# Attention scores in column halves, gate logits in column quarters, and a different schedule of bulk transfers, in a fused attention and mixture-of-experts kernel

## The chip, the cores and the metric

The kernel runs on one core of one Trainium2 chip. The metric is the device time of one execution in microseconds (us). A core has five engines that run side by side: TensorE (PE, matrix products; its weight loads are counted apart as PEld), VectorE (DVE), ScalarE (ACT), GpSimd (POOL) and SyncE (SP, which issues transfers and does no arithmetic). Sixteen DMA engines move data between the large memory and the on-chip memory. TensorE takes two instructions for every product, a weight load (LDWEIGHTS) of the stationary operand and a MATMUL that streams the moving operand past it. A product of 32-bit numbers takes two such pairs, which can be seen from the counts: 256 score products are 512 MATMUL and 512 LDWEIGHTS records in the profile.

## The reference, cut to what matters

```python
# attention: 4 batches, 8 heads, 768 positions, 64 numbers per head, 8 memory slots
for c in range(24):                       # chunks of 32 queries
    keys = mem_k ++ k[32c-16 : 32c+40]    # clipped to the sequence
    a = softmax(q[32c : 32c+32] @ keys.T / 8)
    x[chunk] = a @ (mem_v ++ v[32c-16 : 32c+40])
# experts: x is (3072, 512); 8 experts, 512 -> 1024 -> 512
logits = x @ w_gate
expert = argmax(logits); gate = softmax(logits)[expert]
for e in range(8):
    tok = tokens of expert e; if more than 80, keep the 80 with the largest gate
    out[tok] = gate[tok] * (relu(x[tok] @ w1[e]) @ w2[e])     # all other rows are zero
```

At most 640 of the 3072 output rows are not zero, so the kernel first writes zeros to all rows and later overwrites the chosen ones.

## The kernel before, in words

**Attention.** The work is 32 units. A unit is one pair of heads and one half (384 queries) of the sequence of one batch. Four units make a round: 384 tokens with all 512 numbers. One pass of the loop at line 852 computes, in this order on TensorE: the scores of the *next* unit (`scores`, line 773), a transposition of a key or query pair that is needed later (`turn_k`, `turn_q`), one step of the ranking of an earlier round (`later`), the transposition of the last unit's result (`turn_x`), and the products with the values (`values`, line 351, in 32-column pieces). The scores of a unit are two mask products (line 779) and 4 groups x 2 heads of products with 64 rows, 128 columns of weights and 96 moving columns (line 786). ScalarE takes their exponential (line 794).

**Ranking.** After every fourth unit, `Ranks.steps` gives a list of 11 small steps that are spread over the next passes. The first ones are the gate: `weigh` (line 387, four products that give partial logits per 128 numbers, then a copy by ScalarE, line 417), `logits` (line 422, three products that add up the partial logits), `gates`. For the last round `early` (line 810) computes the logits straight from the transposed results as they appear.

**Experts.** `run_experts` (line 997) gathers the 80 rows of each expert by an indirect transfer that POOL issues (line 1008), transposes them, and does `up` (line 1043) and `down` (line 1057) for each expert: 64 float products each, in 64-column halves of the weights, then scales and scatters the result (`store`, line 1111).

**Transfers.** SP issues nearly all transfers, in program order. In each pass it issues the loads of keys, queries and values (values six passes ahead), every fourth pass a store of a round's results, and then two *pieces* of bulk data of 256 KB: weights (`slow`) or zeros (`nothing`). Weights of an expert's layer are 8 pieces. Nine layer buffers exist; the layers 0, 1, 3, 4 and 2 (the last into the room that keys and queries used) are loaded in the loop, 40 pieces, and all 24 pieces of zeros too. Bulk starts at pass 4. After the loop `paced` issues the other layers; at most six pieces are in flight, so each piece waits for the sixth before it. `in_order` pins the order of every engine to the order of the program.

## Time and profile before

| | |
|---|---|
| three timed runs | 250.19, 251.43, 253.89 us (median 251.43) |
| profiled execution | 248.27 us, of which the span from first to last instruction is 246.5 us |
| attention (to the last transposition of a result) | ends at 138.4 us of the span |
| ranking of the last round, first expert's input | 138.4 to 150.9 us |
| experts | 150.9 to 246.5 us; last product at 240 us |
| bulk weights after the loop | 88 pieces of 256 KB, issued from 138.1 to 218.8 us |

The page gives busy time, shares and counts of each engine; the groups of instructions give for each line the count, the summed busy time and the mean of one in ns, and what the engine waited for just before. A wait on "issue" is a wait for which the profile shows no semaphore. The timeline gives start and duration in us. In a window's line stand the width, then for each engine the busy time and in brackets the number of instructions, the TensorE clock (1.00 is full), the share of the DMA engines and the rate in GB/s. Queue 8 ("instruction") carries the instructions themselves, in transfers of 16,384 bytes each.

### The profile page before, as it was taken

The numbers are of one execution on the slowest core, as the hardware profiler recorded it, in microseconds if no ns is written. First come the engines' busy times: TensorE is split into PE (matmuls) and PEld (weight loads), VectorE is DVE, ScalarE is ACT, GpSimd is POOL, SyncE is SP. The second block draws the span as 40 slices with busy tenths as digits, with TensorE's granted clock in tenths as the row PEclk, the third lists the DMA queues.
The fourth block names the chain that finished last, engine by engine and source line by source line (L and its number), as shares of the span: only waits on it lengthen the run. The fifth ranks groups of instructions, "written<-read, shape, count | busy, mean of one in ns | idle before, by whom it ended". The sixth has DMA issues, their size and how long they took to land. (4 is left out here: it accounts for less than half of the span.)

```text
span 246.5 us, 11417 instructions
## 1 busy us (share of the span) xinstructions
PE 228.3 (93%) x4976; PEld 200.6 (81%) x4976; DVE 105.5 (43%) x288; ACT 81.8 (33%) x198; POOL 80.5 (33%) x182
## 2 busy tenths in 40 slices
PE   5979999999999999999899999969799997999980
PEld 3857889798888788888778889959799996999970
DVE  3333447758579477585555862000112111110240
ACT  2245555665555573665545301100000101010000
POOL 2454947537275182450412147300101010110111
PEclk9999999999999999999999889989999999999996
DMA  6999999999999999999999899999999998890101
GB/s 205 284 283 298 279 296 325 340 370 321 341 364 330 376 331 334 370 278 329 302 305 372 264 363 307 295 333 298 311 335 313 358 288 284 277 332 28 32 29 37
DMA packets 69879, 70.97 MB, mean 288 GB/s; under 512 B 38204, under 2 KB 46396, under 8 KB 69820
## 3 DMA queue, kind: packets, MB, share of 16 engines
q1 hardware_dynamic: 67836, 67.17, 87.4%
q0 software_dynamic: 1024, 2.62, 3.5%
q8 instruction: 41, 0.67, 1.2%
q10 hardware_dynamic: 960, 0.36, 0.6%
q14 instruction: 18, 0.15, 0.2%
HBM read 56.24 MB, written 13.89 MB: 285 GB/s over the span
## 5 line engine op out<-in xcount | busy, mean ns | idle before, releaser
L794 ACT ACTIVATE P<-sp 128x384 f32<-128x384 f32 x64 | 27.9, 488 | 29.6 <-PE sp L786 29.6
L1043 PE MATMUL hp<-xn,w 128*64 128x80 f32 x896 | 33.7, 233 | 3.0 <-issue 3.0
L1043 PEld LDWEIGHTS hp<-xn,w 128*64 128x64 f32 x896 | 32.1, 137 | 3.9 <-issue 3.4
L786 PEld LDWEIGHTS sp<-qT,kT 64*128 64x128 f32 x512 | 33.2, 189 | 1.5 <-issue 0.9
L786 PE MATMUL sp<-qT,kT 64*128 64x96 f32 x512 | 33.5, 269 | 0.9 <-ACT qT L316 0.4
L1057 PE MATMUL yt<-hT,w 128*64 128x80 f32 x896 | 34.2, 239 | 0.0
L1057 PEld LDWEIGHTS yt<-hT,w 128*64 128x64 f32 x896 | 33.0, 142 | 1.2 <-issue 1.1
L1047 ACT ACTIVATE hT<-hp 128x320 f32<-128x320 f32 x16 | 7.0, 437 | 70.7 <-PE hp L1043 70.7
L1111 POOL DMA_INDIRECT out_dram<-y,idx_s x7 | 6.4, 917 | 73.0 <-DVE y L1110 73.0
L357 PE MATMUL o<-vw,P 128*32 128x65 f32 x1536 | 28.9, 222 | 0.7 <-issue 0.7
L357 PEld LDWEIGHTS o<-vw,P 128*32 128x32 f32 x1536 | 23.5, 109 | 6.3 <-issue 5.4
L346 DVE COPY kT<-pt 128x480 f32<-128x480 f32 x32 | 19.9, 666 | 16.3 <-PE pt L343 8.2
L268 POOL COPY vw<-mv 8x512 f32<-8x512 f32 x32 | 22.4, 703 | 8.7 <-DMA vw<-in_v_dram 8.7
L1022 DVE COPY xn<-xp 128x320 f32<-128x320 f32 x7 | 3.4, 491 | 39.4 <-PE xp L1020 39.4
L366 DVE TENSOR_TENSOR xr<-o,over_s 128x384 f32<-128x384 f32 x32 | 17.8, 558 | 1.1
L316 ACT COPY qT<-pt 128x384 f32<-128x384 f32 x31 | 16.0, 582 | 4.8 <-PE pt L315 4.8
L377 ACT COPY xT<-xt 128x384 f32<-128x384 f32 x32 | 15.7, 489 | 4.7 <-PE xt L375 4.7
L330 POOL COPY kh<-ld 128x768 f32<-128x768 f32 x15 | 12.3, 822 | 13.7 <-PE more L549 8.3
L375 PE MATMUL xt<-ident,xr 128*128 128x128 f32 x96 | 16.5, 281 | 0.0
L315 PE MATMUL pt<-ident,qh 128*128 128x128 f32 x96 | 15.0, 291 | 1.2 <-DVE kT L346 1.2
L1063 DVE COPY ys<-yt 128x320 f32<-128x320 f32 x7 | 3.4, 492 | 28.7 <-PE yt L1057 28.7
L531 DVE SCALAR_TENSOR_TENSOR less<-gbs,gw,behind 128x384 bf16<-128x384 f32 x21 | 15.0, 745 | 0.0
(162 smaller groups left out, 305.2 us busy)
## 6 DMA issues: line engine op xcount, KB each, us to landing
w<-in_moe_w_dram SPq DMA_DIRECT2D x120, 256.0 KB, 5.2
vw<-in_v_dram SPq DMA_DIRECT2D x60, 128.0 KB, 5.3
ld<-in_k_dram SPq DMA_DIRECT2D x16, 384.0 KB, 5.6
ld<-in_q_dram SPq DMA_DIRECT2D x16, 384.0 KB, 6.4
xd<-xr SPq DMA_DIRECT2D x8, 768.0 KB, 5.8
out_dram<-zero SPq DMA_DIRECT2D x24, 256.0 KB, 4.9
ld<-in_moe_w_dram SPq DMA_DIRECT2D x8, 256.0 KB, 6.0
vw<-in_v_dram SPq DMA_DIRECT2D x4, 96.0 KB, 5.6
```

The lines of the kernel that those rows point to most:

```text
L268: nc.gpsimd.tensor_copy(self.vw[n, f][:MS, :, :, :D], self.mv[b][:, h : h + 2].unsqueeze(2).to_broadcast([MS, 2, NG, D]),)
L315: nc.tensor.transpose(pt[:, t, :], qh[:, t0 + t].rearrange("p e d -> p (e d)"), ident)
L316: out[t0 // 3](qT.rearrange("p (x t) -> p x t", t=T0)[:, :, t0 : t0 + 3], pt.rearrange("p t x -> p x t"))
L346: nc.vector.tensor_copy(win[:, :, :, u0 : u0 + 3], _ap(pt, 0, [pt.ap[0], [JG, G], [1, (WK - MS) // T0], [step, 3]]),)
L357: nc.tensor.matmul(out[32 * i : 32 * i + 32, e, t, :], lhsT=P[e][:, g, CHUNK * c : CHUNK * c + CHUNK], rhs=self.vw[n, f][:, e, g, :], star ...
L366: nc.vector.tensor_tensor(out=xr[:, :, 128 * c : 128 * c + 128].rearrange("p t (e d) -> p e t d", e=2), in0=o[:, :, :, :D], in1=over_s[:, ...
L375: nc.tensor.transpose(xt[:, 128 * t : 128 * t + 128], xr[:, t, 128 * c : 128 * c + 128], ident)
L377: nc.scalar.copy(xT, xt[:, :HT])
L786: nc.tensor.matmul(sp[e][:, g], lhsT=at.kT[n][r, NG * f + g, :], rhs=at.qT[n][r, HT * f + GQ * g : HT * f + GQ * g + GQ], start=False, sto ...
L794: nc.scalar.activation(P[i][e], sp[e], Act.Exp, scale=scale)
L1043: nc.tensor.matmul(hp[j : j + 64, f, :], lhsT=w1[:, c, f1 : f1 + 64], rhs=xns[e][:, c, :], start=c == 0, stop=c == DK - 1,)
L1057: nc.tensor.matmul(yt[j : j + 64, d, :], lhsT=w2[:, f, d * 128 + j : d * 128 + j + 64], rhs=hTs[e][:, f, :], start=f == 0, stop=f == FK - 1,)
```

## The change

1. `scores`: each score product and each mask product is cut into two products with 64 columns of weights each, so that four products (two heads by two column halves) stand side by side.
2. `logits` takes the place of `weigh` and the old `logits`: for each of 3 token groups and 4 parts of the 512 numbers, four products with 32 columns of weights (transposed results) and 8 moving columns (`w_gate`), added up in PSUM. The copy by ScalarE, the tile `lus` and the constant `sel4` go. `gates` becomes a step of its own. `early` is cut into 32-column products in the same way.
3. Pieces have a size now. A layer's `w1` is 4 pieces of 512 KB (4 KB to a partition), `w2` 8 of 256 KB, and the zeros 12 of 512 KB (4 KB to a partition). `paced` counts sizes and keeps at most six units of 256 KB in flight, as before.
4. The bulk in the loop starts at pass 1, with two units a pass; one of six pieces is zeros. Six of the twelve pieces of zeros are left for after the loop, where they are issued ahead of the weights.
5. The lines that queue layer 2 at pass 26 stand twice, so its 2 MB are loaded twice into the same room.
6. Of the gathers, those of experts 1 to 3 are issued at the start of the experts, the others one by one after each `down`.

```diff
+    def paced(piece):
+        size, dma = piece
         dma()
-        pieces.append(list(nc.cur_bb.bb.instructions)[-1])
-        if len(pieces) > 6:
-            tc.add_manual_dep(pieces[-1], pieces.popleft().name, follow, reason="pieces")
+        ins = list(nc.cur_bb.bb.instructions)[-1]
+        last = None
+        while sum(n for n, _ in pieces) + size > 6:
+            last = pieces.popleft()[1]
+        if last is not None:
+            tc.add_manual_dep(ins, last.name, follow, reason="pieces")
+        pieces.append((size, ins))
...
-                lambda c=c, f=f: nc.sync.dma_start(
-                    t[:, c, f : f + 512], src[i // 2, c * 128 : c * 128 + 128, f : f + 512]
-                )
+                (FK // nch, lambda c=c: nc.sync.dma_start(
+                    t[:, c, :], src[i // 2, c * 128 : c * 128 + 128, :]
+                ))
                 for c in range(nch)
-                for f in range(0, DK * F // nch, 512)
...
-        def weigh(self, xTs, lu):
-            gate_parts(xTs, lu)
-            nc.scalar.copy(self.lus, lu[:, :HT])
-
-        def logits(self):
-            lp = self.ps("lp")
+        def logits(self, xTs, lp):
             for t in range(NT):
-                nc.tensor.matmul(
-                    lp[:, E * t : E * t + E], lhsT=self.lus[:, 128 * t : 128 * t + 128], rhs=sel4,
-                    start=True, stop=True,
-                )
+                for c in range(HP):
+                    for j in range(0, 128, 32):
+                        nc.tensor.matmul(
+                            lp[j : j + 32, E * t : E * t + E], lhsT=xTs[c][:, 128 * t + j : 128 * t + j + 32],
+                            rhs=wgc[:, c, :], start=c == 0, stop=c == HP - 1,
+                        )
             self.largest(lp)
...
-            for e in range(2):
-                r = slice(64 * e, 64 * e + 64)
+            quarters = [(e, slice(64 * e, 64 * e + 64), slice(h, h + 64)) for e in range(2) for h in (0, 64)]
+            for e, r, h in quarters:
                 nc.tensor.matmul(
-                    sp[e].rearrange("p g q -> p (g q)"), lhsT=mkey[r, f, :], rhs=mqry[r, f, :],
+                    sp[e][h].rearrange("p g q -> p (g q)"), lhsT=mkey[r, f, h], rhs=mqry[r, f, :],
                     start=True, stop=False,
                 )
             for g in range(NG):
-                for e in range(2):
-                    r = slice(64 * e, 64 * e + 64)
+                for e, r, h in quarters:
                     nc.tensor.matmul(
-                        sp[e][:, g], lhsT=at.kT[n][r, NG * f + g, :],
+                        sp[e][h, g], lhsT=at.kT[n][r, NG * f + g, h],
                         rhs=at.qT[n][r, HT * f + GQ * g : HT * f + GQ * g + GQ], start=False,
                         stop=g == NG - 1,
                     )
...
             if i == NU - 6:
                 slow += W.load(WR0)
-            for _ in range(2 if i >= 4 else 0):
-                bulk = slow if slow and (i >= NU - 6 or i % 4 < 3) else nothing
-                if bulk:
-                    bulk.popleft()()
-            for _ in range(2 if i >= 20 and i % 2 == 0 else 0):
-                if nothing:
-                    nothing.popleft()()
+            if i == NU - 6:
+                slow += W.load(WR0)
+            if i >= 1:
+                due += 2.0
+            while due > 0 and (slow or len(nothing) > 6):
+                turn = slow if slow and (moved % 6 < 5 or len(nothing) <= 6) else nothing
+                size, dma = turn.popleft()
+                dma()
+                due -= size
+                moved += 1
...
-        for e in range(1, E):
+        for e in range(1, 4):
             gather(e)
...
             down(e)
+            gather(e + 4)
```

More of the change, by code (lines that the diff above doesn't have):

```diff
@@ L115 @@
     tok = masks[:, 2 * WK + 2 * HT :].rearrange("p (i m) -> p i m", i=2)
-    wgc = const.tile([128, HP, 32], F32, name="wgc")
-    sel4 = const.tile([128, E], F32, name="sel4")
+    wgc = const.tile([128, HP, E], F32, name="wgc")
     identb = const.tile([128, 128], BF16, name="identb")
@@ L131 @@
     over_s = const.tile([128, NU, 2, NT], F32, name="over_s")
-    zero = const.tile([128, DM], F32, name="zero")
+    zero = const.tile([128, 2 * DM], F32, name="zero")
     xg0 = const.tile([cap, DM], F32, name="xg0")
@@ L160 @@
     pieces = deque()
-    def paced(dma):
+    def paced(piece):
+        size, dma = piece
         dma()
-        pieces.append(list(nc.cur_bb.bb.instructions)[-1])
-        if len(pieces) > 6:
-            tc.add_manual_dep(pieces[-1], pieces.popleft().name, follow, reason="pieces")
+        ins = list(nc.cur_bb.bb.instructions)[-1]
[5 more added lines that the diff above has]
+        pieces.append((size, ins))
     class Weights:
@@ L184, in load @@
             return [
-                lambda c=c, f=f: nc.sync.dma_start(
-                    t[:, c, f : f + 512], src[i // 2, c * 128 : c * 128 + 128, f : f + 512]
-                )
+                (FK // nch, lambda c=c: nc.sync.dma_start(
+                    t[:, c, :], src[i // 2, c * 128 : c * 128 + 128, :]
+                ))
                 for c in range(nch)
-                for f in range(0, DK * F // nch, 512)
             ]
     def zeros():
-        zrows = 128
+        zrows = 256
         return [
-            lambda i=i: nc.sync.dma_start(
-                out[i * zrows : (i + 1) * zrows, :].rearrange("(p r) d -> p r d", p=128),
-                zero.unsqueeze(1),
-            )
+            (2, lambda i=i: nc.sync.dma_start(
+                out[i * zrows : (i + 1) * zrows, :].rearrange("(p r) d -> p (r d)", p=128), zero
+            ))
             for i in range(N // zrows)
@@ L381, in store @@
             nc.sync.dma_start(xd[r * HT : r * HT + HT, :].rearrange("(t p) d -> p t d", p=128), xr)
-    def gate_parts(xTs, lu):
-        for c in range(HP):
-            nc.tensor.matmul(
-                lu[32 * c : 32 * c + 32, :HT], lhsT=wgc[:, c, :], rhs=xTs[c], start=True, stop=True
-            )
     full = [128, NT, E]
@@ L399, in __init__ @@
             tiles = dict(
-                lus=([128, HT], F32), lmax=([128, NT], F32), lg=(full, F32), first=(full, F32),
+                lmax=([128, NT], F32), lg=(full, F32), first=(full, F32),
                 best=([128, NT], F32), el=(full, F32), oh=([128, NT, 4, E], BF16), gw=([128, NT], F32),
@@ L413, in ps @@
             return self.ps_t.tile([128, 512 if kind == F32 else 1024], kind, name=name, tag="t")
-        def weigh(self, xTs, lu):
-            gate_parts(xTs, lu)
-            nc.scalar.copy(self.lus, lu[:, :HT])
-        def logits(self):
-            lp = self.ps("lp")
-            for t in range(NT):
-                nc.tensor.matmul(
-                    lp[:, E * t : E * t + E], lhsT=self.lus[:, 128 * t : 128 * t + 128], rhs=sel4,
-                    start=True, stop=True,
-                )
+        def logits(self, xTs, lp):
+            for t in range(NT):
+                for c in range(HP):
[4 more added lines that the diff above has]
+                        )
             self.largest(lp)
@@ L608, in turn_table, with steps @@
             nc.scalar.copy(self.tabT, tp[: 3 * E, :cap])
-        def steps(self, r, xTs, lu):
+        def steps(self, r, xTs, lp):
             def fifth():
@@ L628, in steps @@
             return [
-                lambda: self.weigh(xTs, lu), lambda: (self.logits(), self.gates()), lambda: None,
+                lambda: self.logits(xTs, lp), self.gates, lambda: None,
                 lambda: (self.spread(), self.parts(r)), fifth, sixth, seventh,
@@ L730 @@
         make_identity(nc, ident)
-        nc.gpsimd.memset(wgc, 0.0)
-        nc.scalar.dma_start(wgc[:, :, :E], moe_w_gate.rearrange("(c p) e -> p c e", p=128))
+        nc.scalar.dma_start(wgc, moe_w_gate.rearrange("(c p) e -> p c e", p=128))
         def for_gates():
@@ L738, in for_gates @@
             by_q = ident.rearrange("p (q r e) -> p r e q", q=4, e=E)[:, 0]
-            nc.vector.tensor_reduce(sel4, by_q, axis=AX, op=Alu.add)
             with nc.allow_low_precision("ones and zeros"):
@@ L770 @@
         units = [(HP * b + c, f) for b in range(B) for f in range(2) for c in range(HP)]
-        P, o, xr, xTs, lus = {}, {}, {}, {}, {}
+        P, o, xr, xTs = {}, {}, {}, {}
         def scores(i):
@@ L809, in early @@
                 for t in range(NT):
-                    nc.tensor.matmul(
-                        lp[:, E * t : E * t + E], lhsT=xTs[HP * (NR - 1) + c][:, 128 * t : 128 * t + 128],
-                        rhs=wgc[:, c, :E], start=False, stop=c == HP - 1 and t == NT - 1,
-                    )
+                    for j in range(0, 128, 32):
+                        nc.tensor.matmul(
+                            lp[j : j + 32, E * t : E * t + E],
+                            lhsT=xTs[HP * (NR - 1) + c][:, 128 * t + j : 128 * t + j + 32], rhs=wgc[:, c, :],
+                            start=False, stop=c == HP - 1 and t == NT - 1,
+                        )
         turns = {0: [("k", 2), ("q", 2)], 1: [("k", 3), ("q", 3)]}
@@ L820 @@
             turns[i + 1] = turns.get(i + 1, []) + [("q", n)]
-        later, done = deque(), deque()
+        later, due, moved = deque(), 0.0, 0
         ranks = Ranks(gt, ps_x)
@@ L873 @@
             if i and i % HP == 0:
-                lus[r] = ps_x.tile([128, 512], F32, name="lu", tag="t")
-                steps = ranks.steps(r - 1, [xTs[i - HP + c] for c in range(HP)], lus[r])
+                lr = ps_x.tile([128, 512], F32, name="lr", tag="t")
+                steps = ranks.steps(r - 1, [xTs[i - HP + c] for c in range(HP)], lr)
                 later = deque(
@@ L908 @@
         assert not slow
-        for dma in nothing:
-            paced(dma)
+        for piece in nothing:
+            paced(piece)
         r = NR - 1
@@ L1160 @@
             at.turn_mem(ps_t.tile([128, 512], F32, name="pm2", tag="t"))
-            for dma in zeros():
+            for _, dma in zeros():
                 dma()
@@ L1210 @@
                     at.store(r, xr)
-                    steps = ranks.steps(r, xTs, ps_l.tile([128, 512], F32, name="lu2", tag="l"))
+                    steps = ranks.steps(r, xTs, ps_l.tile([128, 512], F32, name="lr2", tag="l"))
                     for step in steps[: None if r < NR - 1 else 4]:
@@ L1228 @@
             for i in range(2):
-                for dma in W2.load(i):
+                for _, dma in W2.load(i):
                     dma()
```

## The prediction

> **What bounds the kernel now.** I read the page first (engines, queues, groups), then the timeline of TensorE pass by pass, then windows for the data rate, and last the waits and what came just before each idle stretch of TensorE.

> ```profile
> PE 228.3 (93%) x4976; PEld 200.6 (81%) x4976; DVE 105.5 (43%) x288; ACT 81.8 (33%) x198; POOL 80.5 (33%) x182
> q8 instruction: 41, 0.67, 1.2%
> L786 PEld LDWEIGHTS sp<-qT,kT 64*128 64x128 f32 x512 | 33.2, 189 | 1.5 <-issue 0.9
> L786 PE MATMUL sp<-qT,kT 64*128 64x96 f32 x512 | 33.5, 269 | 0.9 <-ACT qT L316 0.4
> ```

> TensorE is the bound: the next engine is busy half as long. For the scores the weight loads (33.2 us) take as long as the products. In the timeline one pass reads:

> ```profile
> 112.94 0.34 PE L779 MATMUL sp<-masks 64*128 64x384 bf16 x2
> 113.11 1.03 PE L786 MATMUL sp<-qT,kT 64*128 64x96 f32 x16
> 114.07 0.88 PE L315 MATMUL pt<-ident,qh 128*128 128x128 f32 x6
> ...
> 116.01 0.89 PE L357 MATMUL o<-vw,P 128*32 128x65 f32 x48
> ```

> There is no gap: passes follow each other with TensorE full. The few gaps are of one kind, and they matter here:

> ```profile
> 122.82 0.65 PE L357 MATMUL o<-vw,P 128*32 128x65 f32 x30 [0.73 <-issue]
> 162.84 0.35 PE L1043 MATMUL hp<-xn,ld 128*64 128x80 f32 x2 [2.28 <-issue]
> 175.33 0.49 PE L1043 MATMUL hp<-xn,w 128*64 128x80 f32 x7 [1.28 <-issue]
> 206.59 1.47 PE L1043 MATMUL hp<-xn,w 128*64 128x80 f32 x36 [1.74 <-issue]
> ```

> They fall in the middle of a group, and no semaphore is behind them. Counting TensorE's instructions in the trace (loads, products, semaphore instructions, some 10,060), the four gaps stand before numbers 4801, 6337, 6849 and 8385, all 193 above a multiple of 256. Queue 8 has 41 transfers of 16,384 bytes, one for each 256. So **TensorE runs out of instructions**. The trace's records of queue 8 give three times for each block: from its first instruction to the start of the transfer that brings the next block, 2.35 us on average over the 21 blocks of the attention (2.45 in the experts); the transfer, 1.09 us; and, at the four gaps, from its end to the next instruction, 1.46, 1.55, 1.24 and 1.37 us (1.4). A block thus can't be passed in less than about 2.35 + 1.09 + 1.4 = 4.84 us while data traffic is heavy. The work in a block is now 5.77 us in the attention (21 blocks from 18.7 to 139.8 us), so the refill hides; in the experts it is 4.4 to 5 us, and it hides only sometimes.

> ```profile
> 80.00:100.00 20.00, 19.76 (x389) 16.40 (x381) 12.26 (x34) 11.03 (x28) 7.87 (x17) 1.00 1.11 346
> 220.00:230.00 10.00, 10.00 (x280) 9.72 (x277) 1.24 (x2) 0.87 (x2) 1.22 (x2) 1.00 0.21 69
> ```

> The first row (last numbers: DMA share 1.11, 346 GB/s) is heavy traffic. In the second the refill starts 0.0 to 0.8 us after its block begins, not 2.4: the wait is for the data transfers.

> [...] here the six loads of line 422 (0.19 us each, 0.76 us for the six) follow each other at 113 ns. [...] 128 products with 64-column weights in 4.65 us, 36 ns apart.

> **The change part by part**, against the profiled execution (248.3 us; its span is 246.5; the median of the runs is 3.1 us above it, so I add the differences to 251.4).

> *Scores in halves.* Now 16 products of a unit start in (1.03 - 0.19) / 15 = 56 ns steps, the pace of the loads with two row halves in parallel. After, 32 with 96 columns: 36 ns x 96 / 80 = 43 ns for two column halves, 22 ns with both row halves, 0.70 us in place of 0.90. Gain 0.2 us x 32 = 6.4 us (from 0, if the tiles don't load in parallel, to 9). The mask products stay at 0.17 us.

> *Logits in quarters.* Now 0.79 us (line 387 to what follows) plus 0.67 us (line 422) a round. After, 96 products at the 14 ns of line 357's 32-column ones: 1.35 us. At the densest stretch of 256 instructions in the trace, 14.6 ns each, its 192 instructions take 2.8 us. So -0.1 to +1.3 us a round; I take 0. `early`: three parts, 3.06 us, become 1.4: gain 1.5 us, 0.4 of it in the ranking of the last round. ScalarE's copy (0.48 us x 7) lies beside TensorE: 0.

> *Instructions.* Each float product is four, each mask product two. Scores: +8 x 4 + 2 x 2 = 36 a unit, 1152. Logits: 48 products for 7, +164 a round, 1148. `early`: +144. Sum 2444, **9.5 blocks more**, nearly all in the attention: 30.5 blocks where there were 21. Their work is 121.1 - 1 (its gap) - 6.4 - 1.5 = 112 us, 3.7 us a block, which is below the refill. What a block takes is then the larger of the two. As a test, drawing measured refills against the measured work of each block gives 122.0 us for the attention before (121.1 measured) and 65.1 for 12 blocks of experts (65.7 measured). For after it gives 148 us with the refills as they are. But a slower attention moves its data at a lower rate, and the refill shortens: in the first four blocks, near 299 GB/s, it is 2.0 + 1.14 + 1.4 = 4.54 us. At 4.6 us a block 30.5 blocks are 140.3 us: **+19 us** (bounds: -8 if the refill hides, +27 with no relief).

> *Bulk in the loop.* 40 pieces of weights and 24 of zeros become 48 units (8 of them layer 2's second load) and 12: 60 for 64. A pass moves 384 KB of keys or queries, 256 of values, 512 of bulk and 192 of stores, 1.376 MB. In 3.9 us that is 353 GB/s; at 4.4 us 313. So data don't bind if the refill does. SP's second load of layer 2 must wait for the first (landing takes about 6 us); behind it in SP's queue stand only two stores. Bulk in passes 1 to 3 puts 1.5 MB (4 us of traffic) ahead of keys and values, where POOL already waited 3.7 us for keys at 23.7 us: 0 to 2, I take +0.5.

> *Zeros behind.* 88 pieces at 0.916 us each now; layer 14 has landed by 138.1 + 80 x 0.916 + 5.2 = 216.6 us and is needed at 223.5. Twelve units ahead cost 11 us: 4 us late, unless larger packets lift 286 GB/s to the attention's 345 (then on time). I take +2 (0 to +5). They land long before the first scatter (177.8 us).

> *Gathers.* 957 ns of POOL each; the later ones stand behind a scatter that waits for VectorE. Expert 5's is free after the scatter at 178 us and is read at 208: 0.

> Sum: +19 + 0.5 + 2 - 0.5 (`early` in the last ranking, rounded up) = +21; 251.4 + 21 = **272 us**.

> **Rivals.** (a) *Refill as now hidden*, PE bound: if refills came as promptly as at 220 us (0.8 + 1 + 1.4 = 3.2 us, below 3.7), the gain of 6.4 + 1.5 stays and zeros cost 2: 245.5. For it: before, 20 of 21 attention blocks hid theirs. Against: the 4.84 us. It decides below 3.7 us a block. Chance 0.12. (b) *Data rate takes the gain*: a pass of 3.6 us needs 382 GB/s, and 340 was the mean from 40 to 120 us; then attention stays near its length, 248 to 254. Needs short refills too: 0.13. (c) *Late weights*, larger packets slowing the paced stream, refills half hidden: +5 to +9, 256 to 260. 0.12. (d) Forecast, 0.63: 260 to 286; its top has refills without relief, with TensorE's clock halved after long gaps (after the 2.28 us gap line 1057 took 6.29 us, not 4.65). That the loads don't split [...] would show in the counts; it only removes the gain.

> **Numbers.** Two per cent, about what a measurement of this kernel tells from no change, is 246.4 to 256.5 us. Faster: (a) for the most part, 0.11. Same: (b) and a rest, 0.13. Slower: 0.76. Range 248 to 286, which leaves out (a) and the far top; the likeliest alone 260 to 286.

> **What would show it.** Right: about 50 transfers on queue 8; gaps "issue" in most blocks of the attention, some 0.5 to 1.5 us each; score groups of 0.75 to 0.9 us; the last transposition of a result near 158 us; attention's rate near 310 GB/s. Wrong: no such gaps although the counts rose, then (a) or (b), told apart by waits of POOL or TensorE for keys and values; or a wait for weights at line 1043 late in the experts, then (c).

## The result, and the profile after

The changed kernel takes 291.27 us (median; 289.52 to 293.43) against 250.81 (249.89 to 253.89) for the one before on the same chip: a ratio of 1.161, with a 95% interval of 1.150 to 1.171. The forecast was 272 us, 248 to 286. The direction was right, the size was not. Executions of one kernel differ by up to some 5%, part of them being slower at a lower clock (before, in the set of a_merge: 244.29 us at a mean clock of 0.989, 255.59 at 0.950); ratios with an interval, here and below, compare the faster ones. The profiled execution took 289.52 us (span 287.6, mean TensorE clock 0.921 where it had been 0.978). All stages below are in us of the span.

| stage | before | after | difference |
|---|---|---|---|
| attention, to the end of the last transposition of a result | 138.4 | 171.7 | +33.3 |
| ranking of the last round, to the first expert's first product | 12.5 | 13.6 | +1.1 |
| experts, to the last product | 89.1 | 94.8 | +5.7 |
| last scatter and end | 6.5 | 7.5 | +1.0 |

The page of the changed kernel first: engines, the TensorE clock in 40 slices of 7.2 us, the instruction queue.

```profile
PE 234.3 (81%) x6198; PEld 205.1 (71%) x6198; DVE 104.5 (36%) x287; ACT 79.1 (27%) x191; POOL 79.3 (28%) x181
PEclk9999879999959999779789689999999999879996
q8 instruction: 50, 0.82, 1.2%
```

The clock line of the kernel before:

```profile
PEclk9999999999999999999999889989999999999996
```

There are 1,222 more products and 1,222 more weight loads than before, TensorE is busy only 6 us longer, and yet its share fell from 93 to 81%: the added time is mostly not work. There are 50 transfers of instructions in place of 41, as the count of instructions foretold. After's clock line falls to digits of 5 to 8 in five places within the attention (its first 24 digits). The groups and TensorE's waits say where it stood, first after, then (third fence) the waits on "issue" in before's attention:

```profile
L775 PE MATMUL sp<-qT,kT 64*64 64x96 f32 x1024 | 32.9, 266 | 12.4 <-issue 11.8
L775 PEld LDWEIGHTS sp<-qT,kT 64*64 64x64 f32 x1024 | 29.6, 150 | 14.8 <-issue 13.4
```

```profile
PE sp L775 <- issue: 11.8, 6, 4.2
PE lr L413 <- issue: 9.5, 4, 4.4
PE hp L1038 <- DMA w<-in_moe_w_dram: 4.9, 4, 2.3
PE sp L769 <- issue: 4.3, 1, 4.3
PE o L358 <- issue: 4.1, 3, 1.5
```

```profile
PE o L357 <- issue: 0.7, 1, 0.7
PE sp L786 <- issue: 0.2, 1, 0.2
```

Four of the five largest waits are on "issue", in whatever group the 256th instruction falls: all 14 of the attention stand before an instruction of TensorE whose number is 193 above a multiple of 256, as in the kernel before. A *block* is the 256 instructions from one such number to the next. By these lines TensorE stood idle 29.7 us in after's attention, at 14 of 30 blocks, and 0.9 us in before's. Below, a *gap* is measured from the start of a block's last instruction to the start of the next block's first, which takes in some work: by this measure the gaps of over 0.15 us sum to 32.7 us, where they were 1.5. In the timeline (start, duration, the idle time ahead in brackets) one also sees what follows such a gap:

```profile
27.99 0.83 PE L775 MATMUL sp<-qT,kT 64*64 64x96 f32 x32
...
33.72 1.17 PE L775 MATMUL sp<-qT,kT 64*64 64x96 f32 x25 [2.50 <-issue]
...
40.42 0.75 PE L413 MATMUL lr<-wgc,xT 128*32 128x8 f32 x51 [2.05 <-issue]
...
41.42 1.49 PE L775 MATMUL sp<-qT,kT 64*64 64x96 f32 x32
...
154.45 0.99 PE L413 MATMUL lr<-wgc,xT 128*32 128x8 f32 x96
...
160.54 0.42 PE L775 MATMUL sp<-qT,kT 64*64 64x96 f32 x1 [4.15 <-issue]
161.92 1.53 PE L358 MATMUL o<-vw,P 128*32 128x65 f32 x48
163.75 1.49 PE L775 MATMUL sp<-qT,kT 64*64 64x96 f32 x32
```

A group of 32 score products takes 0.83 us at full clock (it was 1.03 for 16), the 96 logit products 0.99. The same group of scores after the 2.05 us gap, and again after the 4.15 us gap, takes 1.49: TensorE runs at half its clock there. The trace's record of the granted clock has six such stretches in the attention, at 33.9, 40.7, 78.2, 119.2, 139.7 and 160.2 us, 3.4 us long twice and 6.8 us four times, 34.1 us together; before there was none in the attention. Half of TensorE's busy time in them is 14.2 us; that is the most they can have cost.

Windows (the last three numbers: clock, DMA share, GB/s) show that the data transfers were dense at times, but had room later:

```profile
60.00:80.00 20.00, 14.90 (x479) 12.38 (x472) 10.62 (x29) 8.79 (x22) 7.61 (x17) 0.96 1.04 326
120.00:140.00 20.00, 17.37 (x507) 14.77 (x507) 10.75 (x30) 8.92 (x22) 6.78 (x16) 0.84 0.53 151
160.00:180.00 20.00, 19.02 (x399) 15.66 (x401) 12.25 (x43) 5.99 (x17) 4.87 (x17) 0.83 0.43 160
```

In the experts two things are new, weights that come late and half clock after them:

```profile
236.09 4.23 PE L1038 MATMUL hp<-xn,w 128*64 128x80 f32 x116 [1.19 <-DMA w<-in_moe_w_dram]
...
248.65 0.36 PE L1038 MATMUL hp<-xn,w 128*64 128x80 f32 x4 [2.26 <-DMA w<-in_moe_w_dram]
249.70 7.11 PE L1038 MATMUL hp<-xn,w 128*64 128x80 f32 x116 [0.69 <-DMA w<-in_moe_w_dram]
```

Between the first and the last product of the experts TensorE is busy 86.0 us where it was 83.4: the second 116 products alone took 2.9 us longer than the first, at half clock. It is idle 8.7 us where it was 5.7: 4.9 for weights and 2.8 on "issue", in place of 5.3 on "issue".

### The profile page after: what moved, and what is told of

The parts are those of the page before. It is cut to its first block, busy times and chain, and to the rows that moved or that the text cites. A ratio compares the mean times of both kernels' runs of the same rounds, so it can differ in the third digit from the quotient of the medians.

```text
span 287.6 us, 13821 instructions
## 1 busy us (share of the span) xinstructions
PE 234.3 (81%) x6198; PEld 205.1 (71%) x6198; DVE 104.5 (36%) x287; ACT 79.1 (27%) x191; POOL 79.3 (28%) x181
## 3 DMA queue, kind: packets, MB, share of 16 engines
q0 software_dynamic: 1024, 2.62, 2.9%
## 5 line engine op out<-in xcount | busy, mean ns | idle before, releaser
L775 PE MATMUL sp<-qT,kT 64*64 64x96 f32 x1024 | 32.9, 266 | 12.4 <-issue 11.8
L1038 PE MATMUL hp<-xn,w 128*64 128x80 f32 x896 | 36.6, 244 | 7.4 <-DMA w<-in_moe_w_dram 4.9
L1038 PEld LDWEIGHTS hp<-xn,w 128*64 128x64 f32 x896 | 34.8, 146 | 8.5 <-DMA w<-in_moe_w_dram 5.8
L775 PEld LDWEIGHTS sp<-qT,kT 64*64 64x64 f32 x1024 | 29.6, 150 | 14.8 <-issue 13.4
L358 PE MATMUL o<-vw,P 128*32 128x65 f32 x1536 | 31.1, 231 | 4.1 <-issue 4.1
L358 PEld LDWEIGHTS o<-vw,P 128*32 128x32 f32 x1536 | 25.3, 115 | 10.7 <-issue 10.7
L446 POOL TENSOR_TENSOR desc<-oh,masks 128x24 bf16<-128x24 bf16 x16 | 3.3, 227 | 66.8 <-DVE oh L438 44.0
L376 PE MATMUL xt<-ident,xr 128*128 128x128 f32 x96 | 18.4, 305 | 0.2 <-DVE xr L367 0.2
L316 PE MATMUL pt<-ident,qh 128*128 128x128 f32 x96 | 17.5, 324 | 1.2 <-DVE kT L347 1.2
L769 PE MATMUL sp<-masks 64*64 64x384 bf16 x128 | 12.3, 374 | 4.3 <-issue 4.3
```

The lines of the kernel that those rows point to most:

```text
L316: nc.tensor.transpose(pt[:, t, :], qh[:, t0 + t].rearrange("p e d -> p (e d)"), ident)
L358: nc.tensor.matmul(out[32 * i : 32 * i + 32, e, t, :], lhsT=P[e][:, g, CHUNK * c : CHUNK * c + CHUNK], rhs=self.vw[n, f][:, e, g, :], star ...
L376: nc.tensor.transpose(xt[:, 128 * t : 128 * t + 128], xr[:, t, 128 * c : 128 * c + 128], ident)
L775: nc.tensor.matmul(sp[e][h, g], lhsT=at.kT[n][r, NG * f + g, h], rhs=at.qT[n][r, HT * f + GQ * g : HT * f + GQ * g + GQ], start=False, sto ...
L1038: nc.tensor.matmul(hp[j : j + 64, f, :], lhsT=w1[:, c, f1 : f1 + 64], rhs=xns[e][:, c, :], start=c == 0, stop=c == DK - 1,)
```

## The experiments

The theory, called R in the expectations: a block of 256 instructions can't be passed faster than its successor is fetched, so the *count* of TensorE's instructions sets the attention's time. The rivals: packets of 4 KB delay the fetch (a_small); the placing of the bulk data costs the time (a_neither, a_inside, a_single, b_behind, a_within); the density of the bursts matters rather than the count (a_spread); column halves or quarters are slow in themselves (c_merge). A kernel whose label begins with a starts from after, with b or c from before. Ratios are against the kernel before on the same chip; where no interval is given, medians are compared. (In one set, one timing of before and one of b_flight4 were above 1,160 us; they are left out of what is said.)

**One part alone: the scores.** Only `scores` as in the change: +1,152 instructions.

```diff
+            quarters = [(e, slice(64 * e, 64 * e + 64), slice(h, h + 64)) for e in range(2) for h in (0, 64)]
...
+                for e, r, h in quarters:
-                        sp[e][:, g], lhsT=at.kT[n][r, NG * f + g, :],
+                        sp[e][h, g], lhsT=at.kT[n][r, NG * f + g, h],
```

> The kernel before with the scores alone in column halves (1152 TensorE instructions more, 4.5 blocks). Theory R: score groups fall from 1.03 to 0.83 us, but 25.5 blocks of 4.4 us of work meet refills of 4.8 us: gaps of 8 to 20 us in the attention, 252 to 265. Rival D: the shorter groups show in the time, 243 to 248.

Measured: 257.83 us, 1.046 (1.036 to 1.056). The attention has 25 blocks of 5.52 us, where it had 20 of 5.72, and 18.4 us of gaps; 13.7 us passed at half clock, which cost 6.8 us at most:

```profile
PE o L357 <- issue: 7.2, 7, 2.4
PE sp L785 <- issue: 4.3, 4, 2.0
```

The score groups are shorter and the kernel is slower.

**One part alone: the logits.** Only `logits` and `early` as in the change, some 1,290 instructions more.

```diff
-            gate_parts(xTs, lu)
...
+                for c in range(HP):
+                    for j in range(0, 128, 32):
+                        nc.tensor.matmul(
+                            lp[j : j + 32, E * t : E * t + E], lhsT=xTs[c][:, 128 * t + j : 128 * t + j + 32],
+                            rhs=wgc[:, c, :], start=c == 0, stop=c == HP - 1,
+                        )
```

> The kernel before with the logits alone (and early) in column quarters: 1292 TensorE instructions more, most of them in seven bursts of 192 in about 1 us. Theory R with the clock (the refill bounds a block[...]): each burst leaves a block of 2 to 3 us of work, a gap of 2 to 4.5 us and in most rounds a half clock; 12 to 28 us slower than before, with more gap for each added instruction than the value pieces showed (38 us for 3072). Refill without the clock: 5 blocks at 1 to 2 us each, 3 to 10 us slower. Rival D: 4 to 5 us faster, the sum of shorter logits.

Measured: 266.78 us, 1.072 (1.058 to 1.086): 26 blocks of 5.55 us, gaps of 20.3 us (the largest 3.54), 20.5 us at half clock, which cost 10.2 at most. With about the same count the logits cost more than the scores. Their gaps are fewer and longer (10, where b_scores has 15 with 2.60 us as the largest) and more time passes at half clock; how much each adds is not separated.

**The count without the change.** Before's value products, each cut in two along its moving columns: the same tiles of the array, the same transfers, 3,072 more instructions.

```diff
-                    for i in range(4):
...
+                    for d in (slice(0, 33), slice(33, D + 1)):
+                        for i in range(4):
...
-                            rhs=self.vw[n, f][:, e, g, :], start=True, stop=True,
+                                rhs=self.vw[n, f][:, e, g, d], start=True, stop=True,
```

> The kernel before with each product with the values cut into 33 and 32 moving columns: the same result, tiles and transfers, 3072 TensorE instructions more (12 blocks) and up to 8 us more of TensorE work. Theory R: 33 blocks at 4.8 us and more, gaps of 25 us or more at block ends, some half clock: 278 to 305. Rival D: only the added work, 250 to 262.

Measured: 285.03 us, 1.159 (1.148 to 1.170). TensorE's own work grew little: the value group takes 1.03 us where it took 0.89, 4.5 us for all 32. The attention grew by 39.2 us: the rest is 30 us of added gaps (31.4 in all, in 32 blocks of 4.85 us), and half clock, 13.7 us of it, which cost 6.2 us at most.

```profile
79.29 1.03 PE L358 MATMUL o<-vw,P 128*32 128x33 f32 x96
```

```profile
PE o L358 <- issue: 12.9, 11, 2.7
```

An edit that has nothing of the change in it but more instructions costs what the whole change costs. **The count suffices.**

**The count given back.** Two value products that share their moving columns become one with 64 columns of weights: 1,024 instructions fewer. Once on before (b_merge), once on before with the scores in halves (c_merge), once on after (a_merge).

```diff
-            for t in range(NT):
+            for pieces in (((0, 2), (10, 2), (4, 2), (6, 2)), ((8, 1), (9, 1), (2, 1), (3, 1))):
...
-                    for i in range(4):
+                    for q0, m in pieces:
...
-                            out[32 * i : 32 * i + 32, e, t, :], lhsT=P[e][:, g, CHUNK * c : CHUNK * c + CHUNK],
+                            out[32 * i : 32 * i + 32 * m, e, t, :],
+                            lhsT=P[e][:, g, CHUNK * c : CHUNK * c + CHUNK * m],
```

> The kernel before, with neighbouring 32-column value products that share their 65 moving columns made into one with 64 columns of weights: 32 TensorE instructions fewer in each pass, 1,024 fewer in all, so 4 blocks fewer; no other work. Theory R (a block of 256 instructions can't be passed in under 4.8 to 5.2 us): before's attention already hides its refills behind 5.7 us of work a block, so little is to be had: 0 to 2 us faster, 245 to 250 where before is 248; queue 8 has about 37 transfers in place of 41, the block in the attention becomes longer than 6 us. Rival P (32-column products run side by side better than 64-column ones): the group of value products gets longer than 0.89 us and the time rises by 2 to 8 us.

> Before, with the merged value products and with the scores in column halves: 1,152 TensorE instructions more for the scores, 1,024 fewer for the values, so nearly the count of before. Theory R: scores in halves cost 11 us alone only through their count; with the count back the shorter groups of scores (1.03 to 0.83 us, 32 times 0.2 us) show, unless the refill or the data rate takes them: 0.975 to 1.005 of before, gaps at block ends under 5 us in the attention. Rival S (something in the column halves themselves, not the count, costs the 11 us): 1.03 to 1.05 of before, as with the scores in halves alone.

> After, with the merged value products: 1,024 instructions fewer, four blocks fewer in the attention (30.5 to 26.5). Theory R (time goes with the count of blocks): 6 to 15 us faster than after, 1.09 to 1.14 of before, half-clock stretches fewer. Rival: if the gaps come from the transfers of after (larger packets, more bulk early) and not from the count, the time stays at 1.15 to 1.17 of before.

Measured: b_merge 249.57 us, 1.016 (1.008 to 1.024); c_merge 246.78, 1.001 (0.997 to 1.006); a_merge 282.66, 1.154 (1.146 to 1.162), before's median being 248.0. In b_merge rival P is right: the value group takes 1.05 us where it took 0.89, which costs 32 x 0.16 = 5 us.

```profile
90.17 1.03 PE L788 MATMUL sp<-qT,kT 64*128 64x96 f32 x16
92.62 1.05 PE L358 MATMUL o<-vw,P 128*64 128x65 f32 x32
```

```profile
93.36 1.05 PE L358 MATMUL o<-vw,P 128*64 128x65 f32 x32
...
95.01 0.83 PE L787 MATMUL sp<-qT,kT 64*64 64x96 f32 x32
```

The first fence is b_merge, the second c_merge. Between them lies only the cut of the scores, and here it makes the kernel *faster*, from 1.016 to 1.001, intervals apart; from before it made it slower, from 1 to 1.046. The edit is the same, the score groups take the same 0.83 us. What differs is the count on which it lands: b_merge has 16 blocks of 7.2 us in its attention, c_merge 21 of 5.8 with 2.6 us of gaps, b_scores 25 of 5.5 with 18.4. That excludes rival S. As c_merge only returns to the time of before, it is no better kernel: what the scores gain the longer value groups take.

In a_merge the attention got 8 us shorter (163.7 for 171.7), although its value groups cost 5 us more: 26 blocks, gaps 23.2 us for 32.7, half clock 23.9 us for 34.1. Theory R's 1.09 to 1.14 was missed: by the ratios (1.154 and 1.161, intervals overlapping) the expected 6 to 15 us can't be told from nothing, while the two spans differ by 8.1 us. The weights are waited for 8.0 us here, 4.9 in after: part of what the attention gives back is late in the experts.

**Density rather than count.** The 192 logit instructions of a round over two passes in place of one.

```diff
-                lambda: self.logits(xTs, lp), self.gates, lambda: None,
+                lambda: (self.begin(lp), self.logits(xTs, lp, (0, 1))),
+                lambda: (self.logits(xTs, lp, (2, 3)), self.largest(lp), self.gates()), lambda: None,
```

> The changed kernel with each round's 48 logit products in two halves of 24, in two passes that follow each other; the same instructions but seven more that clear. Theory R with the clock: the longest gaps (4.4 to 4.5 us behind the bursts) shrink below 3 us and some half clocks go, 278 to 288. If only the count of blocks matters and not how they are packed: within 1% of the change, 288 to 294.

Measured: 295.56 us, 1.186 (1.170 to 1.201), not faster than after. Gaps are 32.4 us, as in after, and the half clock is longer (41.0 us, at most 18.8 of cost), in a profiled execution that was the longest of the four (301.0 us). Spreading the bursts over two passes gained nothing.

**Packets.** After, with the larger pieces issued as transfers of 256 KB again.

```diff
-                (FK // nch, lambda c=c: nc.sync.dma_start(
-                    t[:, c, :], src[i // 2, c * 128 : c * 128 + 128, :]
-                ))
+                (FK // nch, lambda c=c: [nc.sync.dma_start(
+                    t[:, c, f : f + 512], src[i // 2, c * 128 : c * 128 + 128, f : f + 512]
+                ) for f in range(0, DK * F // nch, 512)])
```

> The changed kernel with every bulk piece issued in transfers of 256 KB and 2 KB runs again; products, schedule, bytes and the double load unchanged. Theory R (a block of 256 TensorE instructions can't be passed faster than its refill, and the refill waits longer behind 4 KB runs): the wait from a block's start to its refill falls from the 4 us seen beside large pieces to about 2.4 us, the gaps at block ends in the attention fall from 33 us to under 20, time 262 to 278. Rival C (instruction count alone, whatever the packets): within 2% of the change, 286 to 297. Rival D (moved and larger bulk alone, instruction count has no part): 246 to 258.

Measured: 286.93 us, 1.162 (1.149 to 1.175), gaps of 29.2 us, where theory R with its delay by 4 KB packets had expected under 20 and 262 to 278 us. The size of the packets is not the cause.

**In flight.** Before, with four paced pieces in flight instead of six.

```diff
-        if len(pieces) > 6:
+        if len(pieces) > 4:
```

> The kernel before with at most four pieces of 256 KB in flight after the loop in place of six. If the refill waits behind queued data: the wait from block start to refill in the experts falls from 2.5 to under 1.9 us and the gaps there from 6 to under 3 us; if the rate of weights stays within 5% of 286 GB/s, 1 to 4 us faster, and if the rate falls with the depth (to 230 GB/s or less), 5 to 20 us slower by late weights. If the wait doesn't come from queued data: the wait stays near 2.5 us.

Measured: a median of 267.7 us (262.45 to 267.80; before 247.2). In the experts the fetch started 1.45 us after its block's begin, not 2.49, and the gaps there fell from 6.4 to 1.8 us: it does wait behind the data in flight. But the weights then came late, 10.7 us in all, where before waited for none:

```profile
PE hp L1043 <- DMA w<-in_moe_w_dram: 10.7, 6, 2.8
```

**The schedule of the bulk.** Five kernels. a_neither is after with `scores`, `logits` and `early` as before, so 10,058 instructions; a_single is a_neither with one load of layer 2; a_inside is a_neither with one load and all zeros in the loop; b_behind is before with half of the zeros behind; a_within is after with a_inside's schedule. The edits of a_inside and a_within, and then of b_behind (a_single has only the first two of these lines):

```diff
-            if i == NU - 6:
-                slow += W.load(WR0)
...
-                due += 2.0
-            while due > 0 and (slow or len(nothing) > 6):
+                due += 2.1
+            while due > 0 and (slow or nothing):
...
-                turn = slow if slow and (moved % 6 < 5 or len(nothing) <= 6) else nothing
+                turn = slow if slow and (moved % 3 < 2 or not nothing) else nothing
```

```diff
-                if nothing:
+                if len(nothing) > 12:
                     nothing.popleft()()
```

> The changed kernel with the scores in full columns and the logits in two steps as before, so with TensorE's instructions of before; schedule, packets, double load, zeros and gathers as changed. Theory R: 21 blocks of about 5.7 us of work against refills of up to 6.5 us, gaps at block ends of 3 to 10 us, late weights +3 to +6: 254 to 265. Rival C: few gaps, only late weights: 250 to 257. Rival D: nearly all of the loss is still there, 280 to 293.

> The changed kernel with scores and logits as before, all zeros inside the loop and one load of layer 2; larger pieces and spread gathers stay. Late weights as the cause of what was left without the column pieces: the waits for weights in the experts (11.4 us) fall under 3 us, and with the refill gaps of the attention staying near 5 us the time is 3 to 8 us above before. If larger pieces themselves were the cause: still 10 to 16 us above.

> After, with scores and logits as they were before (as in a_neither) and layer 2 loaded once instead of twice; half of the zeros stay behind the attention. a_neither stood 1.06 above before and waited 11.4 us for weights in the experts. If the zeros moved behind cause that wait: no change, 1.045 to 1.065 of before and 8 to 12 us of waits for weights. If the second load of layer 2 causes it (2 MB more ahead of the paced weights and one load waiting for the other in SP's queue): 1.01 to 1.03, waits of 2 to 5 us.

> The kernel before, with 12 of its 24 pieces of zeros (3 MB) issued after the loop, ahead of the paced weights; TensorE's instructions and all else as before. As put in the prediction: 12 pieces ahead of the weights cost 11 us of transfers, of which 5 to 9 are found again before layer 14 is needed: +2 us (0 to +5), 248 to 253 where before is 248, waits for weights in the experts of 0 to 5 us. Rival Z (the experts have no such slack, the moved bytes come back whole): +7 to +11 us, 1.03 to 1.045 of before, waits for weights of 7 us and more; the rate near the end of the attention falls below 250 GB/s, since less bulk is left there.

> After, with all zeros in the loop and layer 2 loaded once (the schedule that took the kernel with before's products from 1.06 to 1.03 of before). If the schedule costs the same beside the doubled products: 5 to 9 us below after, 1.12 to 1.14 of before, waits for weights under 2 us. If the attention, longer by 33 us, gives the bulk so much room that its placing no longer counts: 1.15 to 1.17, as after, only the 4.9 us of waits traded for others.

Measured: a_neither 261.67 us (257.32 to 264.83; before 246.62), 1.061 by medians, with 6.6 us of gaps in the attention; a_inside 253.54, 1.027 (1.020 to 1.033); a_single 261.31, 1.067 (1.058 to 1.076); b_behind 251.04 (245.09 to 252.21; before 248.66, 244.24 to 251.13); a_within 285.88 (281.29 to 285.97), 1.150 by medians. The waits for weights, of a_neither, b_behind and a_within:

```profile
PE hp L1049 <- DMA w<-in_moe_w_dram: 11.4, 8, 4.1
```

```profile
PE hp L1043 <- DMA w<-in_moe_w_dram: 0.3, 1, 0.3
PE hp L1043 <- SPq L1148: 2.7, 1, 2.7
```

```profile
PE hp L1036 <- DMA w<-in_moe_w_dram: 6.2, 6, 2.1
```

The zeros behind cost about 2 us by themselves, within the scatter of the runs. In b_behind the second wait, at 224.7 us, is put down to SP by the profile, but stands ahead of the same 116 products whose weights are late in after, so that it is probably for weights too: 3.0 us in all, where rival Z had 7 and more. Rival Z falls. The schedule of after as a whole costs more beside the products of before, some 6%, but what in it does is not separated. a_single was to separate the second load and didn't: its waits fell to 4.3 us and its time stayed. Without the second load its bulk is used up before the attention ends, and the DMA engines stand still, while half clock falls on the end of the attention and the ranking (here 120 to 150 us):

```profile
120.00:130.00 10.00, 9.82 (x271) 8.18 (x263) 7.15 (x23) 5.57 (x14) 3.14 (x10) 1.00 0.60 231
130.00:140.00 10.00, 10.00 (x235) 8.31 (x227) 5.00 (x17) 4.80 (x13) 1.47 (x7) 1.00 0.05 17
140.00:150.00 10.00, 10.00 (x57) 8.82 (x55) 5.21 (x19) 1.95 (x6) 2.67 (x8) 0.50 0.87 325
```

In after itself the placing of zeros and layer 2 hardly shows: with a_inside's schedule a_within is at 1.150 against 1.161, its attention is no shorter (174.7 us), and its 6.2 us of waits are no fewer. By these ratios about half of the expected 5 to 9 us is there, within the scatter. The doubled products can be priced in three ways: 0.10 of before's time beside after's schedule (1.161 against 1.061 for a_neither), 0.12 beside a_inside's (1.150 against 1.027), 0.12 as the sum of their two parts alone (0.046 and 0.072). So they make 10 to 12 of the 16 points, and the schedule the rest.

## Why the prediction was wrong in size

- **Bound, and what would show.** The bound was right: 50 transfers on queue 8, waits on "issue" all over the attention, score groups of 0.83 us (0.75 to 0.9 was given). Their size was wrong: 0.5 to 1.5 us was given, in most blocks, and 0.4 to 4.4 us came, 2.1 on average, at 14 of 30 blocks. So were the last transposition (near 158 us; it was 171.5) and the attention's rate (near 310 GB/s; in five of eight windows of 20 us from 20 us on it was 151 to 254). The rivals that keep the gain, (a) and (b), fell with the gaps; (c), late weights, is there, beside the forecast and not in its place.
- **Scores and logits.** The group of scores went from 1.03 to 0.83 us, the 0.2 us forecast from the 36 ns a product of line 1043's 64-column ones; the logits took 0.99 us, not 1.35 to 2.8, as products with 8 moving columns follow each other at 8.6 ns from start to start, not at the 14 ns of the value products. Both gains were real and both lay under the fetch.
- **Blocks and their fetch.** 2,440 instructions more were counted where 2,444 were forecast, 9.5 blocks. The work in a block came to 3.6 us on average, at full clock, where 3.7 was forecast. The fetch, forecast at 4.6 us: from block to start of transfer 2.22, transfer 1.05, to the next instruction 1.4, sum 4.67. The 4.84 us of before is a mean as well and not a least time: the shortest block of before's attention took 4.3 us, that of after's 3.0.
- **The step that failed** is "At 4.6 us a block 30.5 blocks are 140.3 us: **+19 us**". The mechanism was right, the price of a block too low. After's attention took 5.17 us a block (30 blocks in 155.0 us), and 30.5 x 5.17 = 157.7. (The first of them begins 3.6 us earlier than before's, so that the stage grew by 33.3.) Two things stand between 4.6 and 5.17:
  - *A mean in place of the longer of two.* As the prediction says just before, a block takes the longer of its own work and its own fetch. In after the work of a block goes from 1.7 to 5.6 us at full clock, its fetch from 2.2 to 6.6. The longer of the two, block by block and with the half clock taken out, is 5.0 us on average: an estimate from the trace, with 1.4 us for the last part of each fetch. The prediction's drawing of refills against work had done this and gave 148 us, 4.85 a block; the forecast then put the mean fetch of four of before's blocks (4.54, taken as 4.6) in its place.
  - *Half clock.* It had been seen, line 1057 with 6.29 us for 4.65 behind the 2.28 us gap, and was named for the top of (d), without a sum. Of the seven gaps above 2 us in after's attention six have a half-clock stretch at them. Of the 14.2 us that it can have cost, 3.4 lie in blocks that end in a gap, where less work only makes the gap longer, and part of the rest in blocks hardly longer than their fetch. With each fetch as measured the same estimate leaves 4.6 us for it, 0.15 a block (4 to 8 us with 1.56 to 1.24 us for that last part). That 33.3 exceeds the forecast 19 by 14.2 too is chance. In after the clock fell at idle times of 1.91, 2.05 and 2.50 us, though not at one of 2.09. No run takes the half clock away and leaves the gaps, so that the gaps bring it is read from their order in time and not shown.
- **Relief.** "A slower attention moves its data at a lower rate, and the refill shortens": the rate did fall, further than forecast (249 GB/s from 20 us to the attention's end, where it was 329), but the fetch hardly shortened, 4.67 us for 4.84. The bound without relief, +27, was the better guess.
- **Zeros behind, +2 (0 to +5).** For the zeros alone right (b_behind). After has 4.9 us of waits for weights, and the half clock after them adds 2.9; the second load and the larger pieces are in that too. "Bulk in the loop +0.5" is too small beside before's products (a_inside, with all zeros in the loop and one load, is still 2.7% slower than before).
- **Ranking, -0.5.** The ranking became 1.1 us longer: 2.4 us of it is a wait ahead of the first expert's first product, which was not there before and which the profile marks "issue". That product starts right after ScalarE's copy of its input, at 185.3 us; what this copy waited for the profile does not tell.

Sum: +21 forecast, +41.1 measured in the span. Of the 20 us between, 14 are the price of a block in the attention (33.3 for 19), 3.7 the experts beyond the +2, 1.6 the ranking, 1.0 the end; 0.5 goes off, since the bulk's share can't be seen apart from the attention's.

## What to carry to other kernels

Cutting products into smaller tiles costs instructions, and TensorE's instruction stream has a price by the block: compare the work in 256 instructions with the time of their fetch under the kernel's own traffic (here 4.7 us on average) before dividing anything, and do it block by block, as uneven blocks cost more than their mean (here 5.0). Above that price the same edit gains, below it it loses, as the cut of the scores did (from 1.016 to 1.001, and from 1 to 1.046). Where it leaves TensorE idle for some 2 us at a time (six of the seven gaps above 2 us in after's attention had half clock at them), look for half clock after the gaps, and count it only in blocks that are longer than their fetch.
